# Nine row buffers for leftovers, and the second part's work drawn piecewise from one allowance per tile

## The chip, the cores and the metric

The kernel runs on one core of one Trainium2 chip. The metric is device time in microseconds, from the first to the last instruction of the core and the little that lies around them; lower is better.

## The reference

One GraphSAGE layer over a random graph of 12,500 nodes, 800,000 edges (src, dst) and 64 features:

```python
N, deg, D = 12500, 64, 64          # E = N * deg edges
nsum = segment_sum(x[src], dst, N)  # sum of the neighbours' rows
h_neigh = nsum * deg_inv[:, None]
out = x @ w_self + h_neigh @ w_neigh
```

## The kernel before, in words

**Sorting.** An edge becomes one 32-bit key: which pair of 80-node destination groups it goes to (78 pairs), which 128-row block of x it comes from (98 blocks), and the places inside both. The keys lie in 128 partitions and are sorted in each by a network of min/max stages on VectorE (L219 to L248). Then each of the 78 x 98 = 7644 buckets (a destination pair and a source block) is gathered into one partition row of its own. This goes in two parts (37 and 23 buckets for each of 128 partitions): runs are found by counting (L364), gathered through GpSimd's queue (`gather_runs`, L389), and merged by further min/max stages on VectorE (`merge_runs`, L399; its generator yields after every instruction the nanoseconds that it estimates for it, L408). Then windows are found and gathered (`find_and_gather`, L630, 23 counts on VectorE for the second part), and `decode_buckets` (L644) turns 23 windows, four at a time, into the source places `sl` in HBM (L669) and the destination places `dlT` (L678). What does not fit in a bucket's 128 slots is a leftover: the largest such keys are picked with MAX8 (`pieces`, L708) and become 64 rows of places per part (`leftovers`, L713). `tail` (L760) does the last 20 nodes.

**Summing.** `nodes` (L844) is the main loop. It goes over 962 tiles of 8 buckets. For a tile TensorE multiplies 8 one-hot matrices `ohs` with blocks of x into a PSUM tile `ct` (L867, three buffers), ScalarE copies it to `xg` (L877), and two tiles later TensorE multiplies `xg` with destination one-hots `ohd` into the accumulators (L923, 16 matmuls). VectorE makes the one-hots, 28 buckets at a time (L838 and L841, from a 896 KB load `slb`, L836), at least 44 buckets ahead (AHEAD, L57). From tile SHARE = 503 on every second eviction of those that come just before a refill goes to VectorE (L875).

**Leftover rows.** `rest` (L880) is called before the sums of each tile. A pick loads 128 rows of x for one leftover column with an indirect DMA on GpSimd's queue (L887) into one of five buffers `lx`; it is made when fewer than five picks are unused and the use is at most 400 buckets off (in the first six destination pairs) or 160 (later). A use multiplies it into the accumulators (L903).

**Order around the change.** Everything after the sort stands in an order written by hand. `sums_and_merge` (L1126) steps the generators once per tile n of `nodes`: leftovers of part 0 from n = 2; one more run gather in every third tile until n = 93; the merge of the second part by an allowance t, which gets PACE = 420 ns per tile and pays each step's estimate, from n = 8 for two blocks of rows and from RESUME = 100 on for all the rest (L1175 to L1190); after it, find steps in every second tile, unless a pick was made in the tile before (L1192); after these, one decode step per tile (L1197) and the tail in the odd tiles; then the second part's leftovers. The merge's third block needs the last run gathers, since it sorts their rows. All engines execute their own instructions in this order; GpSimd's queue holds the run gathers (each followed by two small fills, L307), the picks, the window gathers, the `sl` stores of the second part and the output stores (L994) of the first node groups.

Of the kernel before, what the change touches and what calls it, by code (L numbers as in the profile page):

```python
# [11 lines left out]
F32 = mybir.dt.float32  # L12
BF = mybir.dt.bfloat16
FH = mybir.dt.float16
# [19 lines left out]
KPRS = (37, 23)  # L34
# [21 lines left out]
SIG = 5.5  # L56
AHEAD = 44  # L57
RESUME = 100
PACE = 420
SHARE = 503  # L60
SHARED = 60
SPLITS = (2912, 4128)
PITCHES = (SPLITS[1], PITCH1 - UPPER1)
# [4 lines left out]
LAG = 4  # L68
READY = 8
SLOT = 1250  # L70
OCT = 6
LEAST = 2 * HN * NDB
LEND = 14

# [187 lines left out]
class Kernel:  # L262
# [381 lines left out]
    def decode_buckets(self, part, v, vp, mps):  # L644

        nc = self.nc
        kpr = KPRS[part]
        c0 = part * NCNT[0]  # L650

        def bases(k, n, m):
            return view(self.c2[part].rearrange("p a k -> p (a k)").bitcast(I32), k, [[1, n], [kpr, 2], [0, m]])

        def split(k, n, vk, _):
            vh = vk.rearrange("p k (h s) -> p k h s", h=2)
            nc.vector.tensor_tensor(vh, vh, bases(k, n, H), op=OP.bitwise_xor)
            w = vp.tile([128, 4, 128], I32, name="w", bufs=2 + 2 * part)[:, :n]
            nc.vector.tensor_scalar(w.bitcast(F32), vk, 1 << 14, None, op0=OP.is_lt, op1=OP.add,
                                    accum_out=self.cnt[:, c0 + k // 4:c0 + k // 4 + 1])  # L660
            nc.vector.tensor_scalar(w, vk, 7, None, op0=OP.logical_shift_right)
            nc.vector.tensor_scalar(vk, vk, 127, None, op0=OP.bitwise_and)
            return w

        def narrow(k, n, vk, w):
            l16 = vp.tile([128, 4, 128], BF, name="l16", bufs=4)
            nc.scalar.activation(l16[:, :n], w, AF.Copy)
# [3 lines left out]
            nc.scalar.activation(l16[:, :n], vk, AF.Copy)  # L671
            return l16

        def turn(k, n, vk, l16):
            ps = mps.tile([128, 4, 128], BF, name="tr", tag="ct", bufs=3)
            for i in range(n):
                nc.tensor.transpose(ps[:, i], l16[:, i], self.idb)  # L677
            nc.scalar.activation(view(self.dlT, BASE[part] + k, [[kpr, 128], [1, n]]),  # L678
                                 ps[:, :n].rearrange("p k r -> p r k"), AF.Copy)
# [16 lines left out]
        nc.vector.tensor_tensor(e, ext, bases(0, kpr, EXT), op=OP.bitwise_xor)  # L696
        f = e.bitcast(F32)
        for h in range(2):
            nc.vector.scalar_tensor_tensor(f[:, :, h], e[:, :, h], float(1 << 14), ext.bitcast(F32)[:, :, h],
                                           op0=OP.is_lt, op1=OP.mult)  # L700
        yield kpr
        top = self.keep.tile([128, PCS, 9], F32, name=f"top{part}")
        nc.vector.memset(top, 0.0)
        self.pieces(f.rearrange("p k h s -> p (k h s)"), kpr * 2 * EXT, top, PCS)
        self.top = top
        yield kpr

    def pieces(self, f, n, top, pcs):  # L708

        for j in range(pcs):  # L710
            self.nc.vector.max(out=top[:, j, :8], in_=view(f, j, [[pcs, len(range(j, n, pcs))]]))

    def leftovers(self, part, mps):  # L713

# [2 lines left out]
        pool = self.fin  # L717
        n = 8 * REST
        top = pool.tile([128, REST, 8], I32, name="ltop")
        self.pieces(self.top.rearrange("p j i -> p (j i)"), PCS * 9, top.bitcast(F32), REST)  # L720
        k = top.rearrange("p j i -> p (j i)")
        yield 1
# [8 lines left out]
        yield 1  # L731
# [4 lines left out]
        nc.vector.scalar_tensor_tensor(q, t, float(HN), q, op0=OP.mult, op1=OP.add)  # L736
        nc.vector.tensor_scalar(t, k, 14, 1, op0=OP.logical_shift_right, op1=OP.bitwise_and)
# [3 lines left out]
        yield 1  # L741
# [18 lines left out]
    def tail(self, mps):  # L760
# [7 lines left out]
        yield  # L768
        yield
        t = pool.tile([128, n], I32, name="tt")  # L770
        s = pool.tile([128, n], I32, name="ts")
        nc.vector.tensor_scalar(s, k, 8, 0x3F80, op0=OP.logical_shift_right, op1=OP.bitwise_and)
# [71 lines left out]
    def nodes(self, pool, aps, mps):  # L844
# [151 lines left out]
    def check(self, pool, mps):  # L996
# [4 lines left out]
        nc.vector.memset(ones, 1.0)  # L1001
        one = pool.tile([128, 1], F32, name="one")
        nc.vector.tensor_reduce(one, self.cnt, axis=mybir.AxisListType.X, op=OP.add)
        ps = mps.tile([1, 1], F32, name="fps", tag="ct", bufs=3)
        nc.tensor.matmul(ps, one, ones, start=True, stop=True)
        nc.vector.tensor_scalar(self.flag, ps, float(E), None, op0=OP.not_equal)

    def general(self):
# [117 lines left out]
    def sums_and_merge(self, es, mps, aps, u1, other, l2, l2b, l2a, va, vp):  # L1126
# [30 lines left out]
        find = decode = tail = None  # L1157
        self.left = {}
        self.picked, self.used = -9, 0
        left, left_at = self.leftovers(0, mps), 2  # L1160
        t = 0
        for n in self.nodes(fin, aps, mps):
            if left and n >= left_at:
                wait = next(left, None)
                if wait is None:
                    left = None
                    if 1 in self.left:
                        self.check(fin, mps)
# [4 lines left out]
            if tail and n % 2:  # L1173
                next(tail, None)
            if merge and n >= 8 and (n >= RESUME or steps < 2 * per):  # L1175
                t += PACE
                while merge and t > 0:
                    dt = next(merge, None)
                    steps += 1
                    if dt is None:  # L1180
                        merge = None
                        self.merged = True
                        assert self.rows is u1
                        l2b.close()
                        vp = vb.enter_context(tc.tile_pool(name="vb", bufs=1))
                        self.windows(1, vp)
                        self.store_rows(2, tc.nc.scalar)
                        find = self.find_and_gather(1, range(KPRS[1]), LAG)
                    else:
                        t -= dt  # L1190
            elif find:
                if n % 2 == 0 and self.picked < n - 1 and next(find, None) is None:  # L1192
                    find = None
                    decode = self.decode_buckets(1, self.v, vp, mps)
                    tail = self.tail(mps)
            elif decode:
                if next(decode, None) is None:  # L1197
                    assert n < 128 * KPRS[0] // 8 - 12
                    decode = None
                    left, left_at = self.leftovers(1, mps), 0  # L1200
        vb.close()
        l2.close()

# [26 lines left out]
```

## Time and profile before

| | us |
|---|---|
| median of three runs | 1882.71 (1881.04 to 1889.39) |
| the profiled execution | 1888.32 |
| its span, first to last instruction | 1886.6 |
| sort and first part, until the first eviction starts | 798.1 |
| main loop, from there to the last eviction's start (1876.0) | 1077.9 |
| VectorE busy over the span | 1667.2 (88%) |
| ScalarE busy | 1169.7 (62%) |
| TensorE busy (matmul) | 980.7 (52%) |
| GpSimd busy | 809.9 (43%) |

The first five rows are times, the last four the sums of the first part of the profile. The shares are means over stages with very different limits: TensorE hardly works in the first 798 us. So the main loop is read stage by stage, and the tile numbers of the stages follow from the order above: the evictions (L877 and L875) are counted, and the steps that each generator makes are counted from the code.

### The profile page before, as it was taken

The page shows a single profiled execution, that of the slowest core. Times are in us where ns is not written, and L with a number is a line of the kernel's source. Part 1 is how long each engine was busy: PE and PEld are TensorE (multiplying, and loading weights), DVE is VectorE, ACT ScalarE, POOL GpSimd, SP SyncE. Part 2 cuts the span into 40 slices and gives each one's busy share as a digit, 9 for nine tenths or more (in the row PEclk, how much of TensorE's full clock was granted, in tenths as well). Part 3 has the DMA queues.
Part 4 walks back from the last instruction along what each step waited for, and adds up shares of the span by engine and source line. Part 5 has one row for each costly group of instructions (what it writes and reads, how often), then busy time and mean ns, then how long its engine had stood idle before and what let it go on. Part 6 is the DMA issues. An engine that isn't in the chain of part 4 may idle for free.

```text
span 1886.6 us, 54681 instructions
## 1 busy us (share of the span) xinstructions
PE 980.7 (52%) x23698; PEld 839.0 (44%) x23698; DVE 1667.2 (88%) x1805; ACT 1169.7 (62%) x1868; POOL 809.9 (43%) x917
## 2 busy tenths in 40 slices
PE   0015100000000000185888888888868989988997
PEld 0003100000000000174777777777757778777886
DVE  6999999999559999797799999998897888888885
ACT  7435128206500032485898888889977877877786
POOL 1000000798889986888713131313552142222321
PEclk9998655555555555598899999999999999999999
DMA  4304100011100012476678877779766888788784
GB/s 153 70 0 100 36 32 7 21 35 38 22 19 9 10 45 79 127 267 194 211 228 240 264 238 262 244 253 329 264 203 228 267 274 264 253 277 254 247 261 144
DMA packets 104805, 305.25 MB, mean 162 GB/s; under 512 B 52945, under 2 KB 60491, under 8 KB 103915
## 3 DMA queue, kind: packets, MB, share of 16 engines
q1 hardware_dynamic: 86347, 277.44, 41.7%
q0 software_dynamic: 17632, 22.17, 8.8%
q8 instruction: 187, 3.06, 0.6%
q10 hardware_dynamic: 576, 2.07, 0.3%
q14 instruction: 63, 0.52, 0.1%
HBM read 282.20 MB, written 19.41 MB: 160 GB/s over the span
## 4 chain that ended last, share of the span: by engine, by line
DVE 42%; PE 25%; POOL 13%; issue 10%; ACT 5%; DMA 4%; DVEq 0%; SPq 0%; ACTq 0%; POOLq 0%
DVE u L456 15%; PE ct L867 13%; POOL u L394 10%; PE acc L923 9%; DVE b L230 6%; DVE a L230 6%; DVE ohd L841 6%; DVE ohs L838 4%; DMA slb<-sl 2%; ACT xg L877 2%; POOL pad L307 2%; POOL lx L887 1%; DVE u L416 1%; PE acc L903 1%; POOL v L620 1%
## 5 line engine op out<-in xcount | busy, mean ns | idle before, releaser
L877 ACT ACTIVATE xg<-ct 128x1024 f16<-128x1024 f32 (+1 forms) x898 | 852.2, 1033 | 187.3 <-PE ct L867 154.8
L867 PE MATMUL ct<-xh,ohs 128*128 128x128 f16 x7644 | 545.4, 224 | 80.3 <-DVE ohs L838 40.0
L867 PEld LDWEIGHTS <-ohs 128*128 128x128 f16 x7644 | 450.2, 100 | 125.6 <-issue 64.2
L394 POOL DMA_INDIRECT u<-d,ix x256 | 374.0, 1461 | 178.8 <-DVE ix L386 135.4
L923 PE MATMUL acc<-ohd,xg 64*128 64x80 f16 x15288 | 405.9, 199 | 64.2 <-issue 48.9
L456 DVE TENSOR_TENSOR u<-u 128x1456 f32<-128x1456 f32 (+51 forms) x314 | 398.1, 1291 | 19.7 <-ACT u L421 13.6
L923 PEld LDWEIGHTS <-xg 64*128 64x128 f16 x15288 | 319.7, 96 | 135.0 <-issue 65.2
L841 DVE TENSOR_TENSOR ohd<-iota,dlT 128x2240 f16<-128x2240 bf16 x273 | 359.8, 1318 | 0.0
L838 DVE TENSOR_SCALAR ohs<-slb,pidx 128x3584 f16<-128x3584 bf16 x273 | 314.7, 1153 | 35.1 <-PE ct L867 16.6
L887 POOL DMA_INDIRECT lx<-xt,lsrc x140 | 231.2, 1652 | 261.6 <-PE acc L903 228.4
L230 DVE TENSOR_TENSOR b<-a 128x608 f32<-128x608 f32 (+44 forms) x124 | 173.8, 1444 | 6.3 <-ACT a L232 2.3
L230 DVE TENSOR_TENSOR a<-b 128x608 f32<-128x608 f32 (+44 forms) x124 | 173.9, 1445 | 4.5
L994 POOL DMA_DIRECT2D out<-o x25 | 23.7, 949 | 339.6 <-DVE o L993 257.6
L384 PE MATMUL stp<-idf,st 128*128 128x128 f32 x2 | 0.9, 445 | 310.7 <-DVE st L382 310.7
L677 PE MATMUL tr<-idb,l 128*128 128x128 bf16 x60 | 8.0, 273 | 263.9 <-ACT l L671 253.2
L384 PEld LDWEIGHTS stp<-idf,st 128*128 128x128 f32 x2 | 0.4, 183 | 311.1 <-issue 311.1
L875 DVE CAST xg<-ct 128x1024 f16<-128x1024 f32 x64 | 78.2, 1223 | 68.3 <-PE ct L867 63.5
L677 PEld LDWEIGHTS <-l 128*128 128x128 bf16 x60 | 4.9, 117 | 267.1 <-ACT l L671 255.7
L421 ACT ACTIVATE u<-u 128x96 f32<-128x96 f32 (+36 forms) x155 | 32.9, 258 | 134.3 <-DVE u L456 71.1
L375 ACT ACTIVATE junka<-b,c 128x132 bf16<-128x132 f32 (+46 forms) x205 | 90.8, 443 | 12.3 <-DVE b L230 5.8
L232 ACT ACTIVATE b<-a 128x1 f32<-128x1 f32 (+21 forms) x52 | 18.7, 379 | 128.1 <-DVE a L230 122.2
L620 POOL DMA_INDIRECT v<-d,ix x60 | 73.8, 1230 | 55.5 <-ACT ix L638 46.1
(160 smaller groups left out, 795.5 us busy)
## 6 DMA issues: line engine op xcount, KB each, us to landing
slb<-sl SPq DMA_DIRECT2D x273, 896.0 KB
u<-d,ix POOLq DMA_INDIRECT x256
xt<-xh SPq DMA_DIRECT2D x1, 3136.0 KB
fo<-own SPq DMA_DIRECT2D x26, 120.0 KB
own<-os SPq DMA_DIRECT2D x12, 256.0 KB
out<-o POOLq DMA_DIRECT2D x24, 120.0 KB
lx<-xt,lsrc POOLq DMA_INDIRECT x140
rd<-dst SPq DMA_DIRECT2D x4, 521.0 KB
```

Source lines behind the costliest of these rows:

```text
L230: nc.vector.tensor_tensor(view(dst, lo + sh, [[st, g], [1, l]]), x, y, op=op)
L375: nc.scalar.activation(junks[0][:, :n], w, AF.Sign, bias=self.c1[:, 0, c:c + 1], accum_out=a)
L394: nc.gpsimd.indirect_dma_start(out=u[:nr, EDGE + p * w:EDGE + (p + 1) * w], out_offset=None, in_=src, in_offset=bass.IndirectOffsetOnAxis( ...
L456: nc.vector.tensor_tensor(view(dst, EDGE + o + out, d), view(src, EDGE + o + x, d), view(src, EDGE + o + x + gap, d), op=op)
L620: self.nc.gpsimd.indirect_dma_start(out=self.v[:, k].bitcast(F32), out_offset=None, in_=flat(self.d2[home(part, k)], 128 * PITCH2[home(par ...
L838: nc.vector.tensor_scalar(s.rearrange("p c s -> p (c s)"), b, self.pidx[:, :1], None, op0=OP.is_equal)
L841: nc.vector.tensor_tensor(d, self.iota[:, None].to_broadcast([128, 14, HN, 2]), ix, op=OP.is_equal)
L867: nc.tensor.matmul(ct[:, i * 128:(i + 1) * 128], cols[i][0], self.xh[:, (b0 + i) % NB].rearrange("p a f -> p (a f)"), start=True, stop=True)
L875: nc.vector.tensor_copy(xg[:, :cnt * 128], ct[:, :cnt * 128])
L877: nc.scalar.activation(xg[:, :cnt * 128], ct[:, :cnt * 128], AF.Copy)
L887: nc.gpsimd.indirect_dma_start(out=x, out_offset=None, in_=self.xt, in_offset=bass.IndirectOffsetOnAxis(ap=self.left[p][1][:, c:c + 1], ax ...
L923: nc.tensor.matmul(acc[h][:, db % OCT * HN:(db % OCT + 1) * HN], xg[r, i * 128:(i + 1) * 128], d[r], start=db % OCT == 0 and sb == 0, stop ...
```

## The change

Five things, which the diff shows without its trivial lines.

1. Nine `lx` buffers in place of five (ROWAHEAD): a pick is made when fewer than nine are unused.
2. One allowance t for merge, find and decode: PACE is 390, t grows in every tile from n = 8 on (except while the merge waits for RESUME), a find step that counts on VectorE takes 500 from it, and a decode step is made when t is positive and pays its own price. Decode starts four tiles after the last find step.
3. Long steps are divided: the steps that follow the last group of `decode_buckets` (xor, two multiplies, 16 MAX8) become seven, one per tile, in place of two; the leftovers' steps are more and two tiles apart for the second part; the tail waits six odd tiles, not two, between its load and its first use; `check` is two steps, one in every eighth tile, after the tail.
4. VectorE shares the evictions from the moment the second part's leftovers are ready (`self.spare`), not from tile 503.
5. `pieces` is a generator.

```diff
-PACE = 420
-SHARE = 503
+PACE = 390
+ROWAHEAD = 9
...
-            yield min(step // 2 * 4, kpr - 1)
+            yield 2300 if step % per == 0 and step // per < len(groups) else 0
...
         nc.vector.tensor_tensor(e, ext, bases(0, kpr, EXT), op=OP.bitwise_xor)
+        yield 1500
         f = e.bitcast(F32)
         for h in range(2):
             nc.vector.scalar_tensor_tensor(...)
-        yield kpr
+            yield 800
...
-        self.pieces(f.rearrange("p k h s -> p (k h s)"), kpr * 2 * EXT, top, PCS)
+        for _ in self.pieces(f.rearrange("p k h s -> p (k h s)"), kpr * 2 * EXT, top, PCS, 4):
+            yield 900
         self.top = top
-        yield kpr
...
-    def pieces(self, f, n, top, pcs):
+    def pieces(self, f, n, top, pcs, per):
         for j in range(pcs):
             self.nc.vector.max(out=top[:, j, :8], in_=view(f, j, [[pcs, len(range(j, n, pcs))]]))
+            if j % per == per - 1:
+                yield
...
-            if len(picked) < self.used + 5 and len(picked) < len(uses) and uses[len(picked)][0] - early <= b0 \
+            if len(picked) < self.used + ROWAHEAD and len(picked) < len(uses) and uses[len(picked)][0] - early <= b0 \
...
-                x = pool.tile([128, 128], FH, name="lx", bufs=5)
+                x = pool.tile([128, 128], FH, name="lx", bufs=ROWAHEAD)
...
-            pend.append(gather(b0, cnt, t >= SHARE))
+            pend.append(gather(b0, cnt, self.spare))
...
+            if n < 8 or (merge and n < RESUME and steps >= 2 * per):
+                continue
+            t += PACE
+            while merge and t > 0:
...
+                    find = self.find_and_gather(1, range(KPRS[1]), LAG)
+                    decode = self.decode_buckets(1, self.v, vp, mps)
+                    ready = 0
+                else:
+                    t -= dt
+            if merge:
+                continue
+            if find and n % 2 == 0 and self.picked < n - 1:
+                k = next(find, None)
+                if k is None:
+                    find = None
+                    tail = self.tail(mps)
+                elif k < KPRS[1] and not on_act2(1, k):
+                    t -= 500
+            if not find:
+                ready += 1
+            if decode and ready > 4 and t > 0:
+                dt = next(decode, None)
+                if dt is None:
+                    decode = None
+                    left, left_at = self.leftovers(1, mps), 0
+                else:
+                    t -= dt
```

More of the change, by code (lines that the diff above doesn't have):

```diff
@@ L719, in leftovers @@
         top = pool.tile([128, REST, 8], I32, name="ltop")
-        self.pieces(self.top.rearrange("p j i -> p (j i)"), PCS * 9, top.bitcast(F32), REST)
+        for _ in self.pieces(self.top.rearrange("p j i -> p (j i)"), PCS * 9, top.bitcast(F32), REST, 4):
+            yield 1 + part
         k = top.rearrange("p j i -> p (j i)")
-        yield 1
         t = pool.tile([128, n], I32, name="lt")
@@ L730, in leftovers @@
         nc.vector.tensor_tensor(s, s, t, op=OP.bitwise_or)
-        yield 1
+        yield 1 + part
         q = pool.tile([128, n], I32, name="lq")
@@ L736, in leftovers @@
         nc.vector.scalar_tensor_tensor(q, t, float(HN), q, op0=OP.mult, op1=OP.add)
+        if part:
+            yield 2
         nc.vector.tensor_scalar(t, k, 14, 1, op0=OP.logical_shift_right, op1=OP.bitwise_and)
@@ L740, in leftovers @@
         nc.vector.tensor_tensor(z, z, q, op=OP.add)
-        yield 1
+        yield 1 + part
         sel = pool.tile([128, 64], F32, name="sel")
@@ L767, in tail @@
         nc.gpsimd.dma_start(k.bitcast(F32), last.rearrange("(p n) -> p n", n=n))
-        yield
-        yield
+        for _ in range(6):
+            yield
         t = pool.tile([128, n], I32, name="tt")
@@ L1003, in check @@
         nc.vector.tensor_reduce(one, self.cnt, axis=mybir.AxisListType.X, op=OP.add)
+        yield
         ps = mps.tile([1, 1], F32, name="fps", tag="ct", bufs=3)
         nc.tensor.matmul(ps, one, ones, start=True, stop=True)
+        yield
         nc.vector.tensor_scalar(self.flag, ps, float(E), None, op0=OP.not_equal)
@@ L1159, in sums_and_merge @@
         self.picked, self.used = -9, 0
+        self.spare = False
         left, left_at = self.leftovers(0, mps), 2
-        t = 0
+        verdict = None
+        t = found = 0
         for n in self.nodes(fin, aps, mps):
@@ L1167, in sums_and_merge @@
                     if 1 in self.left:
-                        self.check(fin, mps)
+                        self.spare = True
                 else:
@@ L1172, in sums_and_merge @@
                 self.gather_runs(1, u1, [runs.pop(0)])
[L1173 to L1192, printed above, removed]
+            if tail and n % 2 and next(tail, self) is self:
+                tail = None
@@ new lines, in sums_and_merge @@
+            if self.spare and not tail and n % 8 == 0 and verdict != self:
+                verdict = verdict or self.check(fin, mps)
+                if next(verdict, self) is self:
+                    verdict = self
+            if n < 8 or (merge and n < RESUME and steps >= 2 * per):
+                continue
+            t += PACE
+            while merge and t > 0:
+                dt = next(merge, None)
+                steps += 1
+                if dt is None:
+                    merge = None
+                    self.merged = True
+                    assert self.rows is u1
+                    l2b.close()
+                    vp = vb.enter_context(tc.tile_pool(name="vb", bufs=1))
+                    self.windows(1, vp)
+                    self.store_rows(2, tc.nc.scalar)
+                    find = self.find_and_gather(1, range(KPRS[1]), LAG)
[3 more added lines that the diff above has]
+                    t -= dt
@@ L1193, in sums_and_merge @@
+            if merge:
[3 more added lines that the diff above has]
+                if k is None:
                     find = None
-                    decode = self.decode_buckets(1, self.v, vp, mps)
                     tail = self.tail(mps)
-            elif decode:
-                if next(decode, None) is None:
+                elif k < KPRS[1] and not on_act2(1, k):
+                    t -= 500
+            if not find:
+                ready += 1
@@ L1198, in sums_and_merge @@
+            if decode and ready > 4 and t > 0:
+                dt = next(decode, None)
+                if dt is None:
                     assert n < 128 * KPRS[0] // 8 - 12
@@ L1200, in sums_and_merge @@
                     left, left_at = self.leftovers(1, mps), 0
+                else:
+                    t -= dt
+        assert verdict is self
         vb.close()
```

## The prediction

> **What bounds the kernel now.** I read the views in this order: the page's span, busy time by stage, evictions by stage, and the chain of waits inside the two longest stages.
>
> ```profile
> span 1886.6 us, 54681 instructions
> ```
>
> The profiled execution took 1888.32 us, so 1.7 us lie around the span.
>
> ```profile
> core 0: us, PE busy (x) PEld busy (x) DVE busy (x) ACT busy (x) POOL busy (x), PEclk, DMA share, GB/s
> 798.00:929.60 131.60, 102.84 (x2437) 88.37 (x2434) 107.54 (x134) 99.89 (x135) 115.08 (x149) 0.88 0.70 235
> 929.60:1271.80 342.20, 290.33 (x7504) 252.91 (x7500) 338.77 (x318) 299.36 (x356) 85.93 (x49) 0.99 0.76 243
> 1271.80:1352.00 80.20, 71.90 (x1792) 61.34 (x1790) 71.00 (x111) 73.12 (x101) 40.80 (x33) 0.98 0.92 315
> 1352.00:1413.30 61.30, 44.92 (x1038) 36.95 (x1035) 56.84 (x128) 48.47 (x62) 32.82 (x28) 0.94 0.65 208
> 1413.30:1456.20 42.90, 37.09 (x898) 32.73 (x898) 32.12 (x39) 29.31 (x35) 11.93 (x9) 0.92 0.64 212
> 1456.20:1871.50 415.30, 376.31 (x9635) 329.60 (x9636) 345.76 (x372) 330.42 (x361) 117.52 (x79) 0.97 0.82 258
> ```
>
> I cut the main loop where the order of the work changes: tile 100 (the merge resumes), 409 (merge done), 482 (find done), 526 (decode and leftovers done), 560, 955. I counted these from the yields of the generators; the evictions, ScalarE's first and VectorE's below, confirm them (309 tiles, and 40 + 4 = 44), and a window of 16 evictions after the early merge gives a pace without merge work.
>
> ```profile
> 929.60:1271.80 342.20, 290.61 (x309) 0.99 0.76 243
> 1352.00:1413.30 61.30, 38.69 (x40) 0.94 0.65 208
> ...
> 912.70:929.60 16.90, 15.12 (x16) 1.00 0.82 280
> ```
>
> ```profile
> 1352.00:1413.30 61.30, 4.86 (x4) 0.94 0.65 208
> ```
>
> So a tile costs 342.2/309 = 1.107 us in the merge stage, 80.2/73 = 1.099 in the find stage, 61.3/44 = 1.39 in the decode stage, 42.9/34 = 1.26 after it, 415.3/395 = 1.051 late, and 1.056 in the 16. The reader is to see who is full in each: VectorE in the merge stage (338.8 of 342.2) and the decode stage (56.8 of 61.3), TensorE late (376 of 415), GpSimd before tile 100 (115 of 132). The chains of the merge and the late stage say the same:
>
> ```profile
> by line: DVE u L456 28.1%; DVE ohd L841 24.9%; DVE ohs L838 16.2%; issue 15.6%; PE ct L867 4.3%; DMA slb<-sl 3.0%; PE acc L923 2.9%; DVE ohl L895 1.9%; DVE u L416 1.4%; DMA lx<-xt,lsrc 0.9%; DVE o L992 0.7%; PE po L986 0.3%; PE acc L903 0.2
> ```
>
> ```profile
> by line: PE ct L867 46.9%; PE acc L923 32.7%; issue 9.7%; ACT xg L877 3.6%; PE acc L903 2.4%; PE po L986 2.2%; DVE ohd L841 0.6%; DVE xg L875 0.6%; ACT g L928 0.6%; DVE ohs L838 0.6%; DVE o L992 0.1%; DVE ohl L895 0.1%; ACTq L877 0.0%; DVE
> ```
>
> **PACE 390.** The merge's instructions stay the same; they are spread over more tiles. Counted with the code's own estimates, the merge ends at tile 433, not 409; find then takes 73 tiles again (to 506). So the merge stage gets 24 tiles more and the late stage 24 fewer.
>
> ```profile
> L456 DVE TENSOR_TENSOR u<-u 128x1456 f32<-128x1456 f32 (+15 forms) x84 | 124.6, 1486 | 0.5
> L416 DVE TENSOR_TENSOR u<-u 128x656 f32<-128x656 f32 (+2 forms) x4 | 9.2, 2309 | 3.9 <-DMA lx<-xt,lsrc 3.8
> ```
>
> In this stage merge work is 133.8 us, the rest of VectorE 338.8 - 133.8 = 205.0 us, or 0.663 per tile. With 333 tiles VectorE has 133.8 + 333 x 0.663 = 354.6 us; with the 3.4 us that it idled in before, 358.0, or 1.075 per tile. That is above the 1.051 to 1.056 of TensorE and ScalarE, so VectorE still bounds, with little margin. Stage +15.8, late stage -24 x 1.051 = -25.2: together -9.4 at best. If the pace does not improve on 1.107, 333 x 1.107 = 368.6 gives +26.4 - 25.2 = +1.2. With two limits within 2.3% of each other some of the gain is lost to waits for one another; I take **-5**, the middle.
>
> **The divided decode.** Here the allowance does not do what it seems to: in the find stage t gets 390 in each of 73 tiles and pays only 23 x 500, so it stands at about +16 us when decode begins at tile 510, and never comes below 11 us. No piece is ever deferred by it; what spreads the work is that at most one piece is drawn per tile. Groups come every fourth tile as before (tiles 510 to 530), the last long steps are seven pieces in tiles 538 to 544, the leftovers' steps lie in 546 to 564, the tail's one-hots about 550.
>
> ```profile
> L678 ACT ACTIVATE dlT<-tr 128x512 bf16<-128x512 bf16 (+1 forms) x6 | 5.1, 850 | 0.0
> ...
> L671 ACT ACTIVATE l<-v 128x512 bf16<-128x512 int32 (+1 forms) x6 | 3.9, 656 | 0.0
> L667 ACT ACTIVATE l<-w 128x512 bf16<-128x512 int32 (+1 forms) x6 | 3.9, 651 | 0.0
> L711 DVE MAX8 top<-u 128x8 f32<-128x89 f32 (+1 forms) x16 | 3.5, 301 | 0.0
> L659 DVE TENSOR_SCALAR_CACHE_REDUCE w<-v 128x512 f32<-128x512 int32 (+1 forms) x5 | 3.3, 660 | 0.4
> L657 DVE TENSOR_TENSOR v<-v,c 128x512 int32<-128x512 int32 (+1 forms) x5 | 3.3, 658 | 0.0
> L661 DVE TENSOR_SCALAR w<-v 128x512 int32<-128x512 int32 (+1 forms) x5 | 2.3, 456 | 0.2
> L662 DVE TENSOR_SCALAR v<-v 128x512 int32<-128x512 int32 (+1 forms) x5 | 2.2, 443 | 0.2
> L795 DVE TENSOR_SCALAR tm<-wide,tz 128x20 f16<-128x20 f16 x14 | 2.1, 221 | 0.0
> L699 DVE SCALAR_TENSOR_TENSOR u<-u,v 128x713 f32<-128x713 int32 x2 | 1.7, 899 | 0.0
> L696 DVE TENSOR_TENSOR u<-v,c 128x1426 int32<-128x1426 int32 x1 | 1.6, 1633 | 0.0
> ...
> L772 DVE TENSOR_SCALAR ts<-tk 128x14 int32<-128x14 int32 x1 | 0.2, 175 | 3.0 <-DMA tk<-d 3.0
> ```
>
> A group is 0.66 + 0.66 + 0.46 + 0.44 = 2.2 us of VectorE, six make 13.3; xor, multiplies and MAX8 are 1.6 + 1.7 + 3.5 = 6.8. The stage's sum is a check: 56.84 - 44 x 0.663 - 4.86 (evictions) = 22.8, and 2.2 for the group that ran just before the stage: 25 us in all, of which 5 (the one-hots 2.1, the leftovers) come after tile 545 now. So in the 39 tiles from 506 to 545 VectorE has 39 x 0.663 + 20 = 45.9 us; ScalarE 39 x 0.94 (290.6/309) + 9.8 (48.47 - 38.69, the three copies above and two g) = 46.5; TensorE 41.0. Two engines are equally full; in the find stage ScalarE at 73.1 of 80.2 was as full as such a stage got, so I take 50. The wait of 3.0 us for the tail's load goes too: six odd tiles are over 12 us. The next 39 tiles (to 584) are late tiles, 41.0, and I leave 3 us of aftermath, where before it was 42.9 - 34 x 1.051 = 7.2. Together 94, against 61.3 + 42.9 = 104.2 for the same 78 tiles: **-10**. At best 46.5 + 41 = 87.5, -17; at worst 0, since no VectorE work is removed.
>
> The granted clock (the column after the engines) behind the decode stage and in the early stall:
>
> ```profile
> 1405.00:1425.00 20.00, 15.88 (x348) 14.28 (x350) 14.27 (x30) 10.08 (x14) 0.00 (x0) 0.82 0.38 140
> 881.00:898.00 17.00, 7.16 (x123) 5.35 (x123) 1.45 (x3) 2.06 (x3) 13.55 (x26) 0.60 0.27 67
> ```
>
> The aftermath goes with a clock of 0.82, the early stall with 0.60. The Trainium skill (TensorE: Matmul & The Clock Gate, Part 1) says that TensorE falls to half its clock after an idle window of about 3.4 us and needs as long a busy one to come back; the two rows agree. By that rule no 3 us of aftermath would be left once TensorE is fed evenly, and the sum would be 3 us lower.
>
> **Sharing from 567 on.** 55 evictions on VectorE in place of 64. The first nine lay in stages that are counted above without them; the 16 tiles at 1.056 show that ScalarE alone can hold the late pace. Price 0; if it cannot, 22 tiles (545 to 567) at 1.099, +1.
>
> **Nine buffers.** Of 140 picks only 6 to 10 (six to nine in the code's order, which now come at tiles 19 to 33, not 55 to 73) are moved by much; later picks are bounded by the 160 buckets, about 20 tiles ahead in both, but for a few in the last third (14 to 18 before).
>
> The groups of two windows (846 to 929, 882 to 899), the waits before 985, and GpSimd's rows in order of time:
>
> ```profile
> L394 POOL DMA_INDIRECT u<-d,ix x27 | 39.5, 1465 | 5.5 <-issue 5.5
> ```
>
> ```profile
> L394 POOL DMA_INDIRECT u<-d,ix x7 | 6.6, 948 | 1.4 <-issue 1.4
> ```
>
> ```profile
> PE acc L903 <- DMA lx<-xt,lsrc: 14.9, 1, 14.9
> ...
> DVE u L416 <- DMA lx<-xt,lsrc: 3.8, 1, 3.8
> ```
>
> ```profile
> 823.48 2.94 POOL L394 DMA_INDIRECT u<-d,ix  x1 [0.15 <-issue]
> ...
> 833.92 2.85 POOL L394 DMA_INDIRECT u<-d,ix  x1 [0.15 <-issue]
> ...
> 861.47 2.75 POOL L394 DMA_INDIRECT u<-d,ix  x1 [0.30 <-issue]
> ...
> 864.79 1.36 POOL L394 DMA_INDIRECT u<-d,ix  x1 [0.15 <-issue]
> ...
> 880.46 1.36 POOL L394 DMA_INDIRECT u<-d,ix  x1 [0.15 <-issue]
> ...
> 925.87 1.86 POOL L394 DMA_INDIRECT u<-d,ix  x1 [0.31 <-issue]
> ```
>
> The sixth pick stood behind eleven run gathers, and TensorE waited 14.9 us for it. That wait goes. But 12 picks stand ahead of the last run gather (tile 93) in both kernels, so GpSimd's queue is as long as before, and it hardly idles; the merge at tile 100 already waited 3.8 us for it. ScalarE's and VectorE's merge instructions then hold up the evictions and one-hots behind them. What is late next is thus this wait, which grows by what the first one loses: **0**. A few microseconds less (-3) if TensorE's backlog was part of it. More, because gathers ran faster while VectorE idled (0.948 against 1.465 us): 11 gathers and picks x 0.52 = +6, but VectorE's idle time now lies at the end of the queue, where it helps the same.
>
> The Trainium skill (SBUF - State Buffer, Who interferes with whom) says that GpSimd is locked out of its port for the whole of a VectorE operation in a two-port mode, copies and tensor_scalar among them. The 0.948 agrees. By the rule alone, without the idle time that moves, the sum would be 6 us higher.
>
> **Sum.** -5 - 10 + 0 = -15. The profiled execution would take 1888.3 - 15 = 1873.3 and the median 1882.7 - 15 = **1867.7 us, say 1868**.
>
> **The rivals.** A measurement of this kernel tells about 0.5% (9.4 us) from no change: faster is below 1873.3, slower above 1892.1.
> - *ScalarE and TensorE cannot go faster than the find stage's 1.099 while ScalarE evicts alone.* Merge: 333 x 1.099 - 342.2 - 25.2 = -1.4; decode -8 at most: 1873 to 1874. For it: the find stage is slow though VectorE idles 9 us of it. Against: DMA share 0.92 there, 0.76 in the merge stage, and the 16 tiles.
> - *Decode keeps its excess*, since its VectorE work is all there and one-hots wait behind every piece: only -5, 1878.
> - *Slower: run gathers starved behind the port.* Place: GpSimd's queue between 861 and 928 (25 gathers and 7 picks in 67 us). From 823 to 834 gathers started every 3.45 us (four, first and last above). At that spacing the queue takes 32 x 3.45 = 110 us, +43, and the result is 1911. It cancels the gain from a mean spacing of (67 + 15)/32 = 2.6 on. For it: VectorE no longer stops at 881. Against: the nine gathers from 864.79 to 880.46, with VectorE still running, came every 15.67/8 = 1.96 us.
>
> **How the numbers follow.** Forecast 0.60 (faster); the first rival 0.15 and the second 0.13 (both within 0.5%); the third 0.08 and mishaps in the order that I do not see 0.04 (slower). The best ends together, -9.4 - 17 - 3, give 1853; the second rival with half of the queue's price up to tile 100 gives 1878 + 10 = 1888. I set 1852 to 1888.
>
> **What would show it.** Evictions per stage: 333 tiles in 358 to 365 us between tile 100 and 433, VectorE still over 96% busy; tiles 506 to 584 in about 94 us, no clock below 0.9 there; no wait of TensorE on `lx` near 880, but a wait of 15 to 20 us at L416 or L421 on a run gather at tile 100, which would again begin the merge stage near 930. I am wrong if tile 100 comes at 915 (early gain, time below 1855) or at 945 and later.

## The result, and the profile after

The changed kernel takes 1865.6 us (median of 4 runs, 1865.4 to 1874.1), the kernel before 1882.6 (4 runs, 1881.0 to 1889.4): a ratio of 0.9916 [0.9891, 0.9942], or -17 us. The profiled executions, on which the prediction was built, differ by 14.2 us (1888.3 and 1874.1); the forecast was -15. The total is right by luck: two of its terms erred by more than 10 us each, in opposite directions.

The profile after is cut at the same turns of the work: the merge resumes (tile 100, then a stall up to tile 101), merge done (433), find done (506), decode done (545), 584, 955. The `diff` moved the lines by 5: L867 of before is L872, L877 is L882, L887 is L892, L903 is L908, L923 is L928. First the page's span; then the busy time by stage.

```profile
span 1872.4 us, 54706 instructions
```

```profile
core 0: us, PE busy (x) PEld busy (x) DVE busy (x) ACT busy (x) POOL busy (x), PEclk, DMA share, GB/s
798.00:911.80 113.80, 99.61 (x2433) 85.92 (x2430) 107.32 (x133) 99.10 (x135) 101.27 (x129) 0.94 0.79 267
911.80:927.40 15.60, 2.15 (x38) 1.54 (x34) 1.44 (x3) 1.54 (x5) 10.61 (x21) 0.67 0.22 54
927.40:1280.70 353.30, 312.78 (x8042) 273.27 (x8043) 352.72 (x333) 319.24 (x377) 97.08 (x50) 0.97 0.79 252
1280.70:1359.60 78.90, 70.18 (x1755) 60.72 (x1752) 70.80 (x107) 72.75 (x100) 46.92 (x33) 0.98 0.92 314
1359.60:1408.90 49.30, 41.80 (x1000) 36.14 (x1000) 45.15 (x82) 47.06 (x62) 25.12 (x24) 0.97 0.70 240
1408.90:1453.20 44.30, 37.83 (x969) 32.60 (x968) 39.79 (x83) 34.97 (x41) 19.61 (x15) 0.96 0.87 260
1453.20:1857.10 403.90, 355.85 (x9071) 313.12 (x9068) 325.46 (x352) 311.23 (x340) 101.93 (x75) 0.96 0.80 247
```

The reader is to see four things: the stall has moved into a stretch of its own (TensorE 2 of 15.6 us busy); VectorE fills the merge stage (352.7 of 353.3); the two decode stretches have no gap and a granted clock of 0.97 and 0.96; and the last stretch costs 403.9/371 = 1.089 us per tile, where before it was 1.051. Against the terms of the forecast:

| stage (tiles before / after) | before | after | at equal tiles | forecast |
|---|---|---|---|---|
| up to the end of the merge (0-409 / 0-433) | 472.7 | 482.0 | +9.3 - 24 x 1.051 = -15.9 | -5 |
| find (73 tiles) | 80.2 | 78.9 | -1.3 | 0 |
| 78 tiles with decode (482-560 / 506-584) | 104.2 | 93.6 | -10.6 | -10 |
| late (371 tiles; before 371 x 1.051) | 390.0 | 403.9 | +13.9 | 0 |
| sum | | | -13.9 | -15 |

By tiles, the changed kernel is 5.9 us ahead when tile 101 is evicted (927.4 against 933.3), 27.5 at tile 584, and 14.4 at the end: 13 us are given back late.

The waits between 795 and 985 in the profile after, and the chain of waits of its late stretch (1453.2 to 1857.1) by line:

```profile
DVE u L416 <- DMA u<-d,ix: 15.4, 1, 15.4
ACT u L421 <- DMA u<-d,ix: 14.1, 1, 14.1
```

```profile
by line: PE ct L872 44.5%; PE acc L928 32.3%; issue 12.6%; ACT xg L882 3.6%; PE po L991 2.4%; PE acc L908 2.4%; ACT g L933 0.9%; DVE ohs L843 0.6%; DVE xg L880 0.3%; DVE ohd L846 0.3%; ACTq L882 0.0%; DVEq L998 0.0%
```

The wait of 14.9 us on `lx` near 880 is gone (two shorter ones, of 3.2 and 4.4 us at 901 and 917, stand in its place), and the one on a run gather at tile 100 is there, as forecast. Late, TensorE still bounds, but "issue", time in which it waits for nothing that the profile shows, is 12.6% of the chain (before 9.7%, in the prediction's row). The packet records, further down, show what it is.

### The profile page after: what moved, and what is told of

It is laid out like the page before. It is cut to its first block, busy times and chain, and to the rows that moved or that the text cites. A ratio compares the mean times of both kernels' runs of the same rounds, so it can differ in the third digit from the quotient of the medians.

```text
span 1872.4 us, 54706 instructions
## 1 busy us (share of the span) xinstructions
PE 981.5 (52%) x23698; PEld 844.3 (45%) x23698; DVE 1657.6 (89%) x1796; ACT 1176.1 (63%) x1877; POOL 810.3 (43%) x917
## 4 chain that ended last, share of the span: by engine, by line
DVE 33%; PE 26%; POOL 14%; issue 9%; ACT 4%; DMA 3%; DVEq 0%; ACTq 0%; SPq 0%; POOLq 0%
PE ct L872 14%; DVE u L456 14%; POOL u L394 10%; PE acc L928 10%; DVE ohd L846 5%; DVE ohs L843 4%; DVE b L230 3%; DVE a L230 3%; ACT xg L882 3%; DMA slb<-sl 2%; POOL pad L307 2%; POOL lx L892 1%; DVE u L416 1%; PE po L991 1%; PE acc L908 1%
## 5 line engine op out<-in xcount | busy, mean ns | idle before, releaser
L882 ACT ACTIVATE xg<-ct 128x1024 f16<-128x1024 f32 x907 | 860.7, 1046 | 158.7 <-PE ct L872 136.0
L872 PE MATMUL ct<-xh,ohs 128*128 128x128 f16 x7644 | 545.4, 224 | 74.6 <-DVE ohs L843 37.6
L872 PEld LDWEIGHTS <-ohs 128*128 128x128 f16 x7644 | 451.9, 100 | 117.5 <-issue 54.0
L394 POOL DMA_INDIRECT u<-d,ix x256 | 365.8, 1429 | 175.8 <-DVE ix L386 132.3
L928 PE MATMUL acc<-ohd,xg 64*128 64x80 f16 x15288 | 402.8, 200 | 69.8 <-issue 44.7
L456 DVE TENSOR_TENSOR u<-u 128x1456 f32<-128x1456 f32 (+51 forms) x314 | 397.4, 1289 | 8.7 <-ACT u L421 2.6
L928 PEld LDWEIGHTS <-xg 64*128 64x128 f16 x15288 | 319.2, 96 | 138.2 <-issue 67.2
L892 POOL DMA_INDIRECT lx<-xt,lsrc x140 | 235.0, 1679 | 106.0 <-PE acc L908 67.5
L421 ACT ACTIVATE u<-u 128x96 f32<-128x96 f32 (+36 forms) x155 | 33.0, 259 | 145.6 <-DVE u L456 70.0
L880 DVE CAST xg<-ct 128x1024 f16<-128x1024 f32 x55 | 67.3, 1223 | 62.4 <-PE ct L872 62.3
```

Of the source, the lines that this page charges most:

```text
L394: nc.gpsimd.indirect_dma_start(out=u[:nr, EDGE + p * w:EDGE + (p + 1) * w], out_offset=None, in_=src, in_offset=bass.IndirectOffsetOnAxis( ...
L456: nc.vector.tensor_tensor(view(dst, EDGE + o + out, d), view(src, EDGE + o + x, d), view(src, EDGE + o + x + gap, d), op=op)
L872: nc.tensor.matmul(ct[:, i * 128:(i + 1) * 128], cols[i][0], self.xh[:, (b0 + i) % NB].rearrange("p a f -> p (a f)"), start=True, stop=True)
L880: nc.vector.tensor_copy(xg[:, :cnt * 128], ct[:, :cnt * 128])
L882: nc.scalar.activation(xg[:, :cnt * 128], ct[:, :cnt * 128], AF.Copy)
L892: nc.gpsimd.indirect_dma_start(out=x, out_offset=None, in_=self.xt, in_offset=bass.IndirectOffsetOnAxis(ap=self.left[p][1][:, c:c + 1], ax ...
```

## Experiments

Ratios are to the kernel before, run beside each group of experiments, with 95% intervals. The groups ran on different chips (before's median 1886.4, 1877.9 and 1879.3), so ratios are compared, not times. Stage times come from one profiled execution each.

**The parts alone.** First the buffers, in the kernel before:

```diff
-            if len(picked) < self.used + 5 and ...
+            if len(picked) < self.used + 9 and ...
-                x = pool.tile([128, 128], FH, name="lx", bufs=5)
+                x = pool.tile([128, 128], FH, name="lx", bufs=9)
```

> The kernel before with nine row buffers and nothing else. My theory: the early wait of TensorE for the sixth row load (14.9 us near 880) goes, but comes back at tile 100, where the merge waits for the last run gather, some 15 us in place of 3.8; tile 101 is passed within 6 us of before, and the median is -3 us (between -7 and +3) against before. Rival (the stall was worth its length): tile 101 comes 15 us earlier and the median is 14 to 16 us lower. Rival (gathers starved): tile 101 later than before by 5 us or more.

Measured 1899.5 us, 1.0066 [1.0035, 1.0097]. Tile 101 is evicted at 932.8 (before 933.3), behind a wait of 16.5 us at L416: the early stall only moves, as argued. But the median rises by 12.4 us, where 3 us less was expected: tiles 584 to 955 take 402.6 us (before 390.8), which the prediction had priced at no change.

```diff
-PACE = 420
+PACE = 390
```

> The kernel before with PACE 390 and nothing else (merge done at tile 433, decode in tiles 507 to 536 undivided, sharing from 503). My theory: the merge stage runs at about 1.07 us per tile in place of 1.10 with VectorE still over 96% busy, the decode stage keeps its excess, median -5 us (between -10 and 0). Rival (the tiles cannot go faster than 1.10 while ScalarE evicts alone): 0 to +2. Rival (pace is the whole gain): -15.

Measured 1866.4 us, 0.9916 [0.9886, 0.9946]: this constant alone does as much as the whole change, three times the forecast. The merge ran at 328.5 us for tiles 101 to 409 (before 338.5), and tiles 0 to 101 took 127.6 us (134.2).

The decode, leftovers and tail of the change, without its other parts:

```diff
-PACE = 390
+PACE = 420
-ROWAHEAD = 9
+ROWAHEAD = 5
-            pend.append(gather(b0, cnt, self.spare))
+            pend.append(gather(b0, cnt, t >= 503))
```

> The changed kernel with PACE 420, five row buffers and sharing from tile 503, so that only the divided and later decode, leftovers and tail are new (decode in tiles 486 to 520). My theory: the 78 tiles from 482 take about 94 us in place of 104, median -10 us (between -14 and -5) against before. Rival (VectorE's work is all still there, so the excess stays): within 3 us of before.

Measured 1871.5 us, 0.9923 [0.9893, 0.9952]; tiles 482 to 560 take 94.4 us (before 104.2), the forecast size. The three parts alone are -15.8, -14.5 and +12.4 us, together -18 against the measured -17: within intervals of 5 to 6 us on each side, they add up.

**The early stall.** The changed kernel, with the merge resumed 12 tiles later:

```diff
-RESUME = 100
+RESUME = 112
```

> The changed kernel with RESUME 112 in place of 100, so that twelve tiles run while the last run gathers are made; the merge then ends at tile 445 and the sharing begins 12 tiles later. My theory (the early gain was turned into the wait at tile 100, which is GpSimd's queue): that wait falls from 15 us to under 4 and the median is 8 to 12 us below the changed kernel. Rival (VectorE's total up to the end of the second part is what counts, and it is as full as before): VectorE then has the same work in the same time, and the median is within 3 us of the changed kernel.

Measured 1866.7 us, 0.9887 [0.9848, 0.9927]. The wait on the run gather is gone, but TensorE waits 10.9 us for row loads (longest 7.1; after 7.6 and 4.4) and VectorE 5.8; tile 130 comes at 955.6 (after 957.6), and by tile 300 nothing is left. This fits a GpSimd queue whose length is late wherever the wait shows. The ratio's interval overlaps that of the changed kernel (0.9891 to 0.9942), so the 8 to 12 us of the theory are not shown.

**Nine buffers.** The changed kernel with five, then the kernel before with nine buffers behind the old gate of five:

```diff
-ROWAHEAD = 9
+ROWAHEAD = 5
```

> The changed kernel with five row buffers in place of nine, and nothing else. Theory (nine buffers let GpSimd make its row loads in runs of seven to ten behind an output store, and TensorE's instruction loads come late behind these): the stage from tile 584 to 955 takes 387 to 391 us in place of 404, no run of row loads longer than five, and the median is 11 to 15 us below the changed kernel, about 1852. Rival (the late stage is slower for another reason, such as the place or the parity of the shared evictions): the stage stays at 400 or more and the median within 4 us of the changed kernel.

Measured 1857.9 us, 0.9866 [0.9825, 0.9907]; tiles 584 to 955 take 382.4 us.

```diff
-                x = pool.tile([128, 128], FH, name="lx", bufs=5)
+                x = pool.tile([128, 128], FH, name="lx", bufs=9)
```

> The kernel before with nine buffers for the rows, but picks still made only when fewer than five are unused: the order of the instructions on every engine is that of before, and only the number of buffers differs. Theory (the buffers themselves, by what GpSimd may do ahead of TensorE, make the runs of loads): tiles 584 to 955 take 400 us or more, median 10 to 15 us above before. Rival (the earlier place of the picks in the order does it): within 3 us of before, 387 to 392 us for the stage.

Measured 1892.5 us, 1.0057 [1.0030, 1.0083]; tiles 584 to 955 take 401.8 us. In its trace each engine has the instructions of before in the same order; only the number of buffers differs. So it is the buffers, not the order of the picks. Over all the profiles this stage takes 382.4 to 390.8 us in the seven with five buffers, and 401.6 to 404.1 in the five with nine whose loads are not spaced (see below): the two do not overlap. The groups of row loads on GpSimd in this stretch (busy us, mean ns, idle before and what ended it), before and with the nine buffers:

```profile
L887 POOL DMA_INDIRECT lx<-xt,lsrc x67 | 105.9, 1581 | 135.9 <-PE acc L903 128.3 <-issue 6.1 <-PE ct L867 1.5
```

```profile
L887 POOL DMA_INDIRECT lx<-xt,lsrc x65 | 95.2, 1465 | 88.9 <-PE acc L903 73.7 <-issue 10.4 <-PE ct L867 4.3
```

With five, GpSimd waits 128 us for TensorE to free a buffer (the matmul L903); with nine, 74 us. What it does instead shows in GpSimd's rows in order of time, before and after, at the same place of the work. GpSimd stands in an output store that waits 8.6 to 9 us for VectorE, and row loads pile up behind it:

```profile
1673.64 0.84 POOL L994 DMA_DIRECT2D out<-o  x1 [8.96 <-DVE o L993]
1674.80 1.61 POOL L887 DMA_INDIRECT lx<-xt,lsrc  x1 [0.30 <-issue]
...
1681.83 1.73 POOL L887 DMA_INDIRECT lx<-xt,lsrc  x1 [1.02 <-PE acc L903]
1688.58 0.94 POOL L887 DMA_INDIRECT lx<-xt,lsrc  x1 [5.01 <-PE acc L903]
```

```profile
1653.96 0.84 POOL L999 DMA_DIRECT2D out<-o  x1 [8.59 <-DVE o L998]
1655.11 1.62 POOL L892 DMA_INDIRECT lx<-xt,lsrc  x1 [0.30 <-issue]
...
1669.94 0.94 POOL L892 DMA_INDIRECT lx<-xt,lsrc  x1 [0.30 <-PE ct L872]
1675.57 0.94 POOL L892 DMA_INDIRECT lx<-xt,lsrc  x1 [4.68 <-PE acc L908]
```

Five buffers let four loads go in 7 us and then make GpSimd wait; nine let nine go back to back in 16 us. In the chain of waits after, an empty stretch of TensorE follows at once, and the longest of the whole stage 6.5 us behind the ninth load:

```profile
1670.79 1.84 issue
1672.63 0.84 PE ct L872 x12
1674.16 1.00 PE ct L872 x16
1675.98 1.00 PE ct L872 x16
1677.42 5.25 issue
```

The trace's records of DMA packets say what "issue" is here. The page's third part has a queue of its own for instructions; in tiles 584 to 955 of each kernel below, 71 or 72 transfers of 16 KB run on it, of 1.0 us each. TensorE's longer gaps lie at them: after, one of 2.6 us begins at 1507.4, a transfer at 1507.5. Of the 32 gaps over 0.3 us that this stage has after, 31 end between 1.1 and 1.75 us behind the end of such a transfer; gaps spread at random would do so in about one case of eight. So in nearly all of this time TensorE waits for its next instructions. The transfers last as long before (1.02 us) as after (1.04), so it is not they that are slower: the gap of 5.25 us above began 2.9 us before its transfer did. Then I counted the row loads that GpSimd started in the 8 us before each transfer, and took the mean of the gaps that end at it where there were three or more (7 to 12 transfers in each kernel), and where there were none (15 to 33):

| kernel | buffers | longest run of loads | mean gap at an instruction transfer, three or more row loads before / none | all gaps over 0.3 us / those ending at a transfer | tiles 584-955 |
|---|---|---|---|---|---|
| before | 5 | 5 | 0.66 / 0.48 us | 32.5 / 30.6 us | 390.8 us |
| only PACE | 5 | 5 | 0.29 / 0.61 | 35.5 / 34.0 | 387.8 |
| changed, five | 5 | 5 | 0.55 / 0.42 | 30.0 / 29.5 | 382.4 |
| after | 9 | 10 | 1.14 / 0.39 | 45.7 / 45.2 | 404.0 |
| before, gate and buffers 9 | 9 | 9 | 1.68 / 0.26 | 47.3 / 46.3 | 402.6 |
| before, buffers 9 | 9 | 9 | 1.78 / 0.41 | 45.8 / 44.9 | 401.8 |

Where no row loads run, the gaps are 0.3 to 0.6 us with either number of buffers; behind three or more loads they are 0.3 to 0.7 us with five buffers and 1.1 to 1.8 with nine. If the runs are the cause, spacing the loads should cure nine buffers. Each load followed by twelve small memsets on GpSimd, in the changed kernel:

```diff
                     in_offset=bass.IndirectOffsetOnAxis(...))
+                if b0 > 1200:
+                    self.pause(12)
```

> The changed kernel with nine buffers, and twelve small fills on GpSimd behind each row load from bucket 1200 on, so that row loads cannot follow each other within 4 us. Theory (runs of loads are what delays TensorE's instruction loads): tiles 584 to 955 take 387 to 394 us in place of 404 and the median falls by 8 to 14 us against the changed kernel, unless the fills hold up VectorE at their shared port by more than they save. Rival (the runs only go along with the slower stage): 400 us or more.

Measured 1874.3 us, 0.9962 [0.9932, 0.9992]; tiles 584 to 955 take 390.4. No two loads lie closer than 4 us, and the gaps that end at an instruction transfer fall to 26.5 us. But a wait of 16.3 us for row loads that are now late takes part of it back, as the waits of this stretch show (us in total, times, longest); and tiles 480 to 584, where pauses delay the tail's loads, take 132.2 us (after 119.0).

```profile
PE acc L910 <- DMA lx<-xt,lsrc: 16.3, 7, 3.9
```

The stage came out as forecast, but the ratio rose instead of falling (0.9916 after). So once more, half as long and only late:

```diff
+                if b0 > 4704:
+                    self.pause(6)
```

> The changed kernel with nine buffers and six small fills behind each row load from bucket 4704 (tile 588) on: loads come at least some 2.5 us apart, the decode stage is left alone. Theory (runs of loads delay TensorE's instruction loads): tiles 584 to 955 take 385 to 393 us in place of 404, and the median falls by 8 to 14 us against the changed kernel. Rival (a run is as harmful when it is a little stretched, or the harm is elsewhere): 400 us or more.

Measured 1849.6 us, 0.9837 [0.9790, 0.9885]: the best of all, with nine buffers. Six memsets of 0.256 us part the loads by 1.5 us; the gaps at instruction transfers come to 32.6 us, as with five buffers. Its late stretch, beside that of five buffers in the changed kernel, and of five and of nine unspaced in the kernel before (the stage table's columns):

```profile
1447.50:1829.10 381.60, 346.00 (x9071) 304.37 (x9064) 326.09 (x353) 310.54 (x340) 202.65 (x466) 0.99 0.81 264
```

```profile
1452.40:1834.80 382.40, 350.39 (x9070) 308.87 (x9062) 324.76 (x352) 310.36 (x340) 113.64 (x77) 0.97 0.82 263
```

```profile
1480.70:1871.50 390.80, 354.56 (x9059) 310.74 (x9056) 324.54 (x351) 310.73 (x341) 115.01 (x77) 0.97 0.81 258
```

```profile
1473.80:1875.60 401.80, 354.39 (x9058) 312.88 (x9056) 324.50 (x351) 310.88 (x340) 104.74 (x75) 0.96 0.81 250
```

GpSimd does 89 us more than with five (202.65 against 113.64) and the stage is no longer: work on an idle engine was free, its bunching was not. The interval lies below that of the changed kernel (from 0.9891) and overlaps that of five buffers.

**What the decode's gain is made of.** The changed kernel with the last steps joined again (xor and both multiplies one step, sixteen MAX8 one step):

```diff
-        yield 1500
...
-            yield 800
+        yield 0
...
-            yield 900
+            pass
+        yield 0
```

> The changed kernel with the last long steps of the decode joined again (xor and both multiplies in one step, 16 MAX8 in one), all else as changed. Theory (dividing spreads VectorE's work, so that one-hots are late by less): tiles 506 to 584 take 2 to 5 us more than in the changed kernel (93.6), median +1 to +5. Rival (the gain of the decode stage comes from the gap before it, the later leftovers and the evictions that no longer fall into it): within 1 us for the stage.

Measured 1871.3 us, 0.9944 [0.9912, 0.9975]; tiles 506 to 584 take 93.3 us, after 93.6. Dividing them did nothing that the stage shows; the ratio is higher than the changed kernel's 0.9916, with overlapping intervals. Next, five buffers and the old start of the shared evictions:

```diff
-            pend.append(gather(b0, cnt, self.spare))
+            pend.append(gather(b0, cnt, t >= 503))
```

> The changed kernel with five row buffers, and the shared evictions begin at tile 503 again, in the midst of the decode. Theory (an eviction that VectorE makes stands behind the decode's pieces in VectorE's queue, and TensorE waits for it): tiles 506 to 584 take 5 to 10 us more than with five buffers alone (86.9), and TensorE's waits for evictions by VectorE come to 7 us or more there. Rival (sharing only moves work from one full engine to another): within 2 us, the waits under 4.

Measured 1866.7 us, 0.9910 [0.9877, 0.9943], where five buffers alone had 0.9866 [0.9825, 0.9907]: higher, but the intervals overlap. Tiles 506 to 584 with five buffers, then with the early sharing too, and a wait of TensorE in that stage of the latter:

```profile
1365.50:1452.40 86.90, 75.33 (x1930) 64.99 (x1928) 84.13 (x163) 81.30 (x102) 41.05 (x36) 1.00 0.76 251
```

```profile
1359.20:1459.00 99.80, 81.73 (x1972) 71.12 (x1974) 96.07 (x175) 76.51 (x95) 43.68 (x35) 0.93 0.70 228
```

```profile
PE acc L928 <- DVE xg L880: 9.0, 4, 2.6
```

VectorE has 12 instructions and 12 us more, ScalarE 5 us less, and the stage is 12.9 us longer: TensorE waits for evictions that VectorE makes among decode's steps. But VectorE was busy for 97% of this stage already (84.13 of 86.90) and is so for 96% of the longer one. So whether an eviction costs by its place in VectorE's queue or simply as more work on a full engine, this run does not part. Last, the tail with its old wait, and the leftovers in as many steps as before and one tile apart, both with five buffers:

```diff
-        for _ in range(6):
+        for _ in range(2):
```

> The changed kernel with five row buffers, and the tail waits two of its steps after its load, as before, not six. Theory (VectorE stood 3.0 us for this load before): VectorE waits for it again, 2 to 4 us, and tiles 506 to 584 take 2 to 4 us more than with five buffers alone (86.9). Rival (the load has landed by then, or VectorE makes the time good): no wait over 1 us, within 1.5 us.

Measured 1856.1 us, 0.9867 [0.9824, 0.9910]; the wait for the tail's load is back (2.6 us), the stage is 2.3 us longer (89.2), the ratio is that of five buffers.

```diff
-            yield 1 + part
+            pass
+        yield 1
...
-        yield 1 + part
+        yield 1
...
-        if part:
-            yield 2
```

> The changed kernel with five row buffers, and the second part's leftovers in as many steps as before, one tile apart. Theory (their 3.5 us of VectorE's work are late tiles' work when spread): tiles 506 to 584 take 1 to 3 us more than with five buffers alone (86.9). Rival (VectorE has caught up by then): within 1 us.

Measured 1854.3 us, 0.9865 [0.9820, 0.9909]; the stage is 93.1 us in its profile (86.9 with five buffers alone), the ratio unchanged. No effect of either on the time was found, and a stage of one profile can evidently differ by some 6 us without one in the median.

## Why the prediction was right in total, and where its steps failed

The sum came out because two errors cancelled: PACE gave 11 us more than its term, and the late stage took 14 us back that no term had.

**PACE: right direction, mis-sized.** The term was -5, its best case -9.4 (the middle that the prediction says it took would be -4.1); the stages up to the end of the merge gave -15.9, PACE alone -15.8 in the median. Over the profiles, tiles 0 to 433 take 477.7 to 487.2 us in the nine at 390, and tiles 0 to 409 with 24 late tiles 490.3 to 498.0 in the four at 420. Two things make it up, -10.4 and -5.5. The merge stage itself: 358.0 us was the price if VectorE loses nothing to waits, and half of the gain was then struck off because two limits lay within 2.3%. After, it took 353.3 us for 332 tiles (1.064), VectorE 99.8% busy: nothing was lost. The step "with two limits within 2.3% of each other some of the gain is lost to waits for one another" failed. And the early merge steps draw PACE too; the prediction counted it only from tile 100 on. In the trace the last of them starts behind 93 evictions after, and behind 83 before. The groups of run gathers from 798 to 930, before, after, and with PACE alone:

```profile
L394 POOL DMA_INDIRECT u<-d,ix x45 | 76.3, 1697 | 8.3 <-issue 8.3
```

```profile
L394 POOL DMA_INDIRECT u<-d,ix x45 | 66.7, 1483 | 8.3 <-issue 8.2
```

```profile
L394 POOL DMA_INDIRECT u<-d,ix x44 | 68.1, 1548 | 8.2 <-issue 8.2
```

The gathers that GpSimd's queue consists of take 0.15 to 0.21 us less each, 8 to 10 us in all, and tiles 0 to 101 take 5.5 to 6.6 us less. That PACE makes this second part is likely, not shown: the nine profiles at 390 (that with RESUME 112 apart) have 124.0 to 130.4 us for tiles 0 to 101, of four at 420 three have 132.1 to 134.3, but that with only nine buffers has 126.3. The third rival, gathers starved every 3.45 us for a time of 1911 us, is refuted.

**Decode: the size is right (-10.6 against -10), the cause only in part.** The stretches were forecast at 50 and 44 us and took 49.3 and 44.3, with no clock below 0.9, so the second rival is out. For the aftermath I had allowed 3 us, where the clock rule (the Trainium skill, TensorE: Matmul & The Clock Gate, Part 1) would leave none; 44.3 - 39 x 1.051 = 3.3 were left, at a clock of 0.96. That the allowance never defers a piece fits the trace: the last long steps follow each other at tiles 537 to 545, forecast 538 to 544; no run leaves out the test `t > 0`. But spreading the last long steps was worth nothing that the stage shows. And the price 0 of "Sharing from 567 on" hid a large part of this term: the decode stage was counted without the evictions that had fallen into it, 4.86 us of VectorE for four of them. Put back with five buffers, they made this stage 12.9 us longer, and the ratio 0.9910 against 0.9866 (the intervals overlap). Yet the decode part alone, still sharing from 503, also had 94.4 for 104.2. So the two gains do not simply add, and how the rest falls to the gap ahead of decode, the tail and the leftovers stays open; two of these, taken back one at a time, moved no median.

**The early stall: right.** Zero was forecast for the buffers there, with a wait of 15 to 20 us at L416 or L421; it was 15.4, and 16.5 with the buffers alone. The merge began at 927.4, "near 930". Read by its letter the line on tile 100 would have misled: that tile was evicted at 911.8, since the stall now stands behind it. What counts is tile 101.

**Nine buffers late: the step that failed.** "later picks are bounded by the 160 buckets, about 20 tiles ahead in both" is true of the order in which the picks are written, and so the late stage was priced at 0. But the order is not the time. The buffers also decide how far GpSimd may run behind a stalled store, and the stage took 13.9 us more. That the buffers do it is shown by the kernel in which only their number changes (+11.0), by five buffers in the changed kernel (-21.5), and by nine spaced ones (-22.3). By the packet records TensorE's gaps at instruction transfers grew by 14.6 us from before to after, which is the whole of it. Why these come late behind runs of row loads is not shown: no view says what an instruction load waits for.

**The first rival,** that no stage goes below 1.099 per tile with ScalarE evicting alone, is refuted: 1.064.

## What to carry to other kernels

A buffer count is not only a question of space: it is the brake on an engine that runs ahead, and where that engine also waits in order for something else, more buffers turn steady transfers into bursts; look at what the bursts delay, and space them before you add buffers. Where two engines share a job such as evictions, the one that is full, or has long steps in its queue, makes the consumer wait, so start sharing after the long steps. And check a forecast by stage, not by its sum: here -16, -11 and +14 met a forecast of -5, -10 and 0.

## What the runs showed of the hardware that was not expected

TensorE's time without a visible reason is time at its instruction loads. In the late stretch after, 72 transfers of 16 KB in 404 us, 31 of its 32 gaps over 0.3 us end 1.1 to 1.75 us behind the end of a transfer. It is not constant: 0.3 to 0.6 us on average where no row load started in the 8 us before, and behind three or more of them 1.1 to 1.8 us with nine buffers and 0.3 to 0.7 with five.

A GpSimd run gather lasted 1.48 to 1.70 us on average in the same 45, by what ran beside it. The Trainium skill (SBUF - State Buffer, Who interferes with whom) lets VectorE's two-port modes block GpSimd and says that tensor_tensor has none, but with both inputs in SBUF contends with GpSimd's reads. The merge steps that PACE spreads are tensor_tensor (L456), and the gathers' mean fell with them; but it also fell to 1.59 us with nine buffers at the old PACE, so no run here settles it.
